# Small softmax operations of a second expert folded and given to GpSimd, its pairs written in another order

## The chip, the cores and the metric

The kernel runs on one core of a Trainium2 chip. A core has a matrix engine (TensorE, PE in the profile), a vector engine (VectorE, DVE), a scalar engine (ScalarE, ACT), a general engine (GpSimd, POOL) and an engine that here only starts DMAs (SyncE, SP). Each works through its own list of instructions in the order in which they were written, and waits for the others by semaphores. PE accumulates in PSUM, eight banks of 512 fp32 columns for 128 partitions. The metric is the device time of one execution in microseconds, lower is better.

## The reference

Three stages follow one another: linear attention, a first expert `h * cos(h)`, and the second expert that the change touches:

```python
def _moe2_ref(x, w_in, w_out, g_ln):          # x: 4608 x 512
    h = x @ w_in                              # 512 x 1024
    e = np.exp(h - np.max(h, axis=-1, keepdims=True))
    sm = e / (np.sum(e, axis=-1, keepdims=True) + 1e-09)
    solu = h * sm
    mu = np.mean(solu, axis=-1, keepdims=True)
    var = np.mean((solu - mu) ** 2, axis=-1, keepdims=True)
    ln = (solu - mu) / np.sqrt(var + 1e-06) * g_ln
    return (ln @ w_out).astype(np.float32)    # 1024 x 512
```

All is fp32, for 4608 tokens. The softmax's division by z, the sum of the exponentials, is never carried out: h times e is normalised as it stands, and the small constants are scaled by the square of z.

## The kernel before

Matrix products in fp32 precision are made from split numbers: each operand is a high part (rounded, ACT's cast at L479) and a low part (what is left, POOL's or DVE's subtraction at L480), and `mm3` (L204 to L206) adds three matmuls. Products of two by two blocks use seven block products instead of eight, with sums of blocks as operands.

The second expert works on 18 pairs of 128-token tiles, u = 0 to 17. For a pair:
- `prep_second` loads x (L1188), makes block sums on POOL (L779) and splits them (L479 on ACT, L480 on POOL).
- `second` (S below) makes h by seven products of six matmuls of 512 columns. `H_SEED[u]` chooses one of three ways to combine the products: by DVE sums (L1231), by DVE operations that add and take the row maximum at once (L1236), and by ACT copies (L1241, L1281, L1288).
- `soft` runs once for each of the two tiles, n = 0 and 1 ("rows"): the negated maximum `nmx` (L1309, DVE), Exp with its sum z (L1314, ACT), h times e with its sum (L1317, DVE), the negated mean `nmp` (L1320, DVE), the square of z (L1324, ACT), the squared deviations with their sum (L1326, ACT), the variance (L1328, DVE), its power -1/2 (L1331, POOL), a product (L1345, POOL) and the normalisation (L1347, ACT).
- `permute` writes the result through DMAs (L1365, SP), `turned` transposes it and splits it (L1392, L1403, L1415, L1416), all on engines beside PE; pairs 0 and 17 have PE transposes.
- `second_out` (O below) makes the output by seven products. Where `O_WIDE[u]` is set and u is under 16, a product is four pairs of matmuls of 512 and 256 columns (L1466, L1468); else it is twelve matmuls of 256 (L204 to L206). ACT copies (L1483, L1500), DVE sums (L1476, L1490, L1496) and POOL sums (L1492) combine them, and DMAs write them out (L1583).

So that PE always has work, the products of S for one pair stand between products of O for a pair two places earlier. In a flow of such pairs an output product's accumulation bank is copied by ACT (`ps<-ps` copies at L1483 and L1500) before PE opens the third output product in the bank that the copy frees or fills.

The order of every engine is not written by hand. Each `add` in the functions notes an operation with its engine, a planned duration, what it reads and writes, and a priority `at`. `Flow.run` then plans them all: it takes the operation that could start first, among those the one of lowest `at`, and calls its function, which issues the instruction. DVE and POOL operations that are not marked `ps` never overlap in that plan. The tables at the head of the file (leads and lags in us, `H_SEED`, `O_WIDE`, `O_SEED`) set the priorities and the forms:

```python
            t = min((t for t in q if start(t) <= s), key=lambda t: (t.at, t.seq))
            q.remove(t)
            ...
            t.fn()
```

The functions are stored as lambdas and run here, after all the `add` calls of all pairs have been made.

Of the kernel before, what the change touches and what calls it, by code (L numbers as in the profile page):

```python
# [53 lines left out]
E2_LEAD, SOFT_AT, SOFT_D, Q_OFF, CP_D = -33.18, -44.29, -15.08, -0.17, 6.96  # L54
# [5 lines left out]
S_A1, S_AL, S_DL, E2_AT, S_BL, ITEM_L, ACC_AT = -19.57, 38.93, 58.24, 168.95, 35.39, 38.61, -6.64  # L60
# [6 lines left out]
PREP_LO, P1_SEED, CHAIN_POOL, H_SEED, O_SEED = (1, 1, 1, 1), (1, 1, 1, 1, 0, 0, 1, 0, 0, 1, 0, 1, 0, 0, 1), (0,), (2, 2, 0, 0, 0, 2, 0, 0, 2, 0, 0, 0, 0, 0, 0, 0, 0, 0), (2, 0, 1, 0, 1, 1, 2, 1, 1, 0, 0, 1, 0, 0, 0, 0, 2, 1)  # L67
STRASSEN = (0, 0, 0, 0, 1, 0, 1, 1, 0, 1, 1, 0, 1, 1, 1)
O_WIDE, MM_W = (0, 0, 1, 0, 0, 1, 1, 1, 1, 0, 1, 1, 0, 1, 0, 0, 0, 1), 0.342
# [123 lines left out]
def tile_kernel(ctx, tc, qkv, tail, g2, w1, w2, gl, out):  # L193
# [1106 lines left out]
    def soft(u, n, at):  # L1300
# [4 lines left out]
        def sm(name):  # L1305
            return buf[name, n]

        if n or H_SEED[u] != 1:
            add("DVE", 0.15, lambda: DVE.tensor_scalar(out=sm("nmx"), in0=sm("mb"), scalar1=-1.0, scalar2=None,  # L1309
                                                       op0=ALU.mult), r=[("mb", n)], w=[("nmx", n)], at=at, ps=True)  # L1310
        else:
            add("DVE", 1.19, lambda: DVE.tensor_reduce(out=sm("nmx"), in_=buf[hk], axis=AX.X, op=ALU.max, negate=True),
                r=[*halves], w=[("nmx", n)], at=at, ps=True)
# [3 lines left out]
        add("DVE", 1.3, lambda: DVE.scalar_tensor_tensor(out=buf[hk], in0=buf[hk], scalar=1.0, in1=buf[ek],  # L1317
                                                          op0=ALU.mult, op1=ALU.mult, accum_out=sm("sp")),
            r=[*halves, ek], w=[hk, ("sp", n)], at=at)
        add("DVE", 0.15, lambda: DVE.tensor_scalar(out=sm("nmp"), in0=sm("sp"), scalar1=-1.0 / FP, scalar2=None,  # L1320
                                                  op0=ALU.mult), r=[("sp", n)], w=[("nmp", n)], at=at, ps=True)


        add("ACT", 0.27, lambda: ACT.activation(out=sm("zz"), in_=sm("z"), func=AF.Square, scale=1e-3,  # L1324
                                               bias=buf["halfpi"][:, 1:2]), r=[("z", n), "tiny"], w=[("zz", n)], at=at)
        add("ACT", 1.24, lambda: ACT.activation(out=buf["junk"], in_=buf[hk], func=AF.Square, bias=sm("nmp")[:, 0:1],  # L1326
                                                accum_out=sm("v")), r=[hk, ("nmp", n)], w=[("v", n), "junk"], at=at)
        add("DVE", 0.16, lambda: DVE.scalar_tensor_tensor(out=sm("v"), in0=sm("v"), scalar=1.0 / FP, in1=sm("zz"),  # L1328
                                                         op0=ALU.mult, op1=ALU.add),
            r=[("v", n), ("zz", n)], w=[("v", n)], at=at)  # L1330
# [12 lines left out]

        if n in NORM_ACT:
            add("POOL", 0.2, lambda: POOL.tensor_tensor(out=sm("nmp"), in0=sm("nmp"), in1=sm("ry"), op=ALU.mult),  # L1345
                r=[("ry", n)], w=[("nmp", n)], at=at, ps=True)
            add("ACT", 1.13, lambda: ACT.activation(out=normed(), in_=plain(), func=AF.Identity, scale=sm("ry")[:, 0:1],  # L1347
                                                   bias=sm("nmp")[:, 0:1]),
                r=[hk, ("nmp", n), ("ry", n)], w=[("nx", n)], at=at)
            return  # L1350
# [587 lines left out]
```

## Time and profile before

| what | value |
|---|---|
| time, median of 3 runs (lowest to highest) | 1195.18 us (1194.14 to 1196.62) |
| the profiled execution, and its span | 1195.32 us, 1193.4 us |
| PE, DVE, ACT, POOL busy, share of the span | 99%, 79%, 72%, 62% |
| granted TensorE clock, mean | 0.998 of full speed |

The second expert's pairs fill about the last 350 us. A busy share is an average over three stages, and the end of a matmul in the profile is modelled, so pauses of PE are read below from the starts of successive matmuls. In the timeline a row has the start, the duration, the engine, the line, the operation and its tiles, and in brackets the idle time before it with the operation that ended it; two rows of equal kind are joined, with x2.

### The profile page before, as it was taken

What the parts mean: (1) busy time and instruction counts of PE and PEld (TensorE: products, weight loads), DVE (VectorE), ACT (ScalarE), POOL (GpSimd) and SP (SyncE); (2) the same over time, 40 slices, a digit from 0 to 9 for tenths busy, and PEclk for the clock granted to TensorE, in tenths of its full rate; (3) what the DMA queues carried; (4) which work ended last, traced back from release to release, by engine and by line L of the source; (5) the groups of instructions that cost most, each with busy time, mean ns of one, the idle gap of its engine ahead of it and who ended that gap; (6) DMA issues with size and microseconds to landing.
All of it is one profiled execution on the core that took longest, in us unless ns stands there. A gap on an engine that the chain in (4) does not pass through costs nothing.

```text
span 1193.4 us, 20361 instructions
## 1 busy us (share of the span) xinstructions
PE 1177.4 (99%) x6678; PEld 1023.4 (86%) x6678; DVE 945.2 (79%) x1631; ACT 861.8 (72%) x1602; POOL 740.8 (62%) x737
## 2 busy tenths in 40 slices
PE   7999999999999999999999999999999999999998
PEld 6788888888999999888888878888898988888898
DVE  6877666666657769789989888887789888989895
ACT  6787777777655746767577758664879878787874
POOL 3377675667534345778477646877567675776732
PEclk9999999999999999999999999999999999999999
DMA  9899999988967987986598569879834342433331
GB/s 321 287 364 330 332 319 326 327 271 302 306 200 215 316 275 228 354 302 219 179 353 313 202 206 336 283 247 333 275 108 117 92 134 79 131 100 100 102 94 54
DMA packets 244394, 281.35 MB, mean 236 GB/s; under 512 B 17984, under 2 KB 169536, under 8 KB 244288
## 3 DMA queue, kind: packets, MB, share of 16 engines
q1 hardware_dynamic: 244288, 280.04, 72.2%
q8 instruction: 53, 0.87, 0.3%
q14 instruction: 53, 0.43, 0.1%
HBM read 184.03 MB, written 79.17 MB: 221 GB/s over the span
## 4 chain that ended last, share of the span: by engine, by line
PE 90%; DVE 5%; SPq 2%; ACT 1%; DMA 1%; issue 1%; POOL 0%; DVEq 0%; ACTq 0%
PE ps L204 26%; PE ps L206 26%; PE ps L205 26%; PE ps L1466 4%; PE ps L709 3%; PE ps L1468 2%; PE ps L591 2%; SPq L1365 1%; PE ps L741 1%; DMA att<-qkv 1%; DMA xf<-px 1%; DVE mid L1084 0%; DVE rxa L480 0%; DVE ps L1392 0%; DVE fconv L1403 0%
## 5 line engine op out<-in xcount | busy, mean ns | idle before, releaser
L204 PE MATMUL ps<-rg,rwo 128*128 128x512 f32 (+2 forms) x752 | 269.6, 359 | 2.0 <-DVE fh L1084 1.1
L206 PE MATMUL ps<-rg,rwo 128*128 128x512 f32 (+2 forms) x752 | 265.7, 353 | 0.0
L205 PE MATMUL ps<-rg,rwo 128*128 128x512 f32 (+2 forms) x752 | 265.5, 353 | 0.0
L204 PEld LDWEIGHTS ps<-rg,rwo 128*128 128x128 f32 x752 | 141.7, 188 | 20.7 <-DVE mid L1084 2.7
L206 PEld LDWEIGHTS ps<-rg,rwo 128*128 128x128 f32 x752 | 141.7, 188 | 16.3
L480 POOL TENSOR_TENSOR rg<-rawp,rg 128x512 fp32r<-128x512 f32 (+1 forms) x84 | 116.8, 1402 | 62.0 <-ACT rg L479 58.4
L205 PEld LDWEIGHTS ps<-rg,rwo 128*128 128x128 f32 x752 | 141.9, 189 | 15.0
L204 PE MATMUL ps<-rxa,rwi 128*128 128x512 f32 (+1 forms) x384 | 144.8, 377 | 0.0
L206 PE MATMUL ps<-rxa,rwi 128*128 128x512 f32 (+1 forms) x384 | 144.3, 376 | 0.0
L205 PE MATMUL ps<-rxa,rwi 128*128 128x512 f32 (+1 forms) x384 | 144.3, 376 | 0.0
L840 DVE SCALAR_TENSOR_TENSOR fh<-ps,fh 128x512 f32<-128x512 f32 (+1 forms) x126 | 81.0, 648 | 45.7 <-ACT fh L838 44.0
L843 ACT ACTIVATE fh<-fh,const 128x512 f32<-128x512 f32 (+1 forms) x156 | 105.1, 689 | 16.7 <-DVE fh L840 15.6
L204 PE MATMUL ps<-rxb,rwi 128*128 128x512 f32 (+1 forms) x288 | 109.4, 380 | 1.9 <-DVE fh L948 0.9
L205 PE MATMUL ps<-rxb,rwi 128*128 128x512 f32 (+1 forms) x288 | 108.4, 376 | 0.0
L206 PE MATMUL ps<-rxb,rwi 128*128 128x512 f32 (+1 forms) x288 | 108.3, 376 | 0.0
L480 POOL TENSOR_TENSOR ws<-fconv,ws 128x512 fp32r<-128x512 f32 x68 | 83.3, 1228 | 38.6 <-ACT ws L479 32.7
L479 ACT CAST rg<-rawp 128x512 fp32r<-128x512 f32 (+1 forms) x144 | 83.3, 597 | 27.3 <-PE ps L206 18.9
L838 ACT ACTIVATE fh<-ps 128x512 int32<-128x512 f32 (+1 forms) x126 | 70.6, 566 | 44.1 <-PE ps L206 41.8
L779 POOL TENSOR_TENSOR sf<-xf 128x256 f32<-128x256 f32 x72 | 65.5, 909 | 30.5 <-DMA xf<-xd 22.8
L204 PEld LDWEIGHTS ps<-rxa,rwi 128*128 128x128 f32 x384 | 72.1, 188 | 12.1 <-ACT ps L963 0.4
L206 PEld LDWEIGHTS ps<-rxa,rwi 128*128 128x128 f32 x384 | 72.1, 188 | 11.7
L205 PEld LDWEIGHTS ps<-rxa,rwi 128*128 128x128 f32 x384 | 72.1, 188 | 10.8
(197 smaller groups left out, 3122.1 us busy)
## 6 DMA issues: line engine op xcount, KB each, us to landing
rwi<-wid SPq DMA_DIRECT2D x66, 512.0 KB, 6.0
rwo<-wod SPq DMA_DIRECT2D x104, 256.0 KB, 4.4
att<-qkv SPq DMA_DIRECT2D x32, 512.0 KB, 6.2
rwo<-wsd SPq DMA_DIRECT2D x32, 512.0 KB, 5.3
fh<-e2n SPq DMA_DIRECT2D x256, 64.0 KB, 2.1
fconv<-w SPq DMA_DIRECT2D x28, 512.0 KB, 5.4
px<-fh SPq DMA_DIRECT2D x42, 256.0 KB, 5.3
xd<-xf SPq DMA_DIRECT2D x18, 512.0 KB, 5.3
```

Of the source, the lines that this page charges most:

```text
L204: PE.matmul(ps, lhsT=lh, rhs=rh, start=start, stop=False, skip_group_check=more)
L205: PE.matmul(ps, lhsT=lh, rhs=rl, start=False, stop=False, skip_group_check=more)
L206: PE.matmul(ps, lhsT=ll, rhs=rh, start=False, stop=stop, skip_group_check=more)
L479: add("ACT", 0.62 if n == 512 else 0.405, lambda: ACT.copy(out=hi(), in_=src()), r=keys, w=hk, at=at)
L480: either(on_dve, n, lambda eng: eng.tensor_tensor(out=lo(), in0=src(), in1=f(hi()), op=ALU.subtract), [*keys, *hk], lk, at)
L591: PE.matmul(buf[bk][e * D:(e + 1) * D, p % 2 * D:(p % 2 + 1) * D], lhsT=k_[:, at_:at_ + D], rhs=k_[:, v_ + at_:v_ + at_ + D], start=(c == ...
L709: PE.matmul(buf[bk][row:row + n, c], lhsT=buf[qs[p]][:, a:a + n], rhs=buf[kvf][:, c], start=True, stop=True)
L779: add("POOL", 0.74, lambda: POOL.tensor_tensor(out=out_(), in0=in0(), in1=in1(), op=fn), r=[*keys, *r], w=w, at=at)
L838: add("ACT", e_(0.6, 0.385, n), lambda: ACT.activation(out=tt().bitcast(I32), in_=h(), func=AF.Copy, scale=INV_2PI, bias=0.25), r=r, w=[tk ...
L840: add("DVE", e_(0.69, 0.418, n), lambda: DVE.scalar_tensor_tensor(out=tt(), in0=h(), scalar=INV_2PI, in1=tt().bitcast(I32), op0=ALU.mult, ...
L843: add("ACT", e_(0.725, 0.509, n), lambda: ACT.activation(out=tt(), in_=tt(), func=AF.Sin, bias=buf["halfpi"][:, 0:1], scale=TWO_PI), r=[tk ...
L1466: PE.matmul(buf[bk], lhsT=hi, rhs=lw_room(b, c // 2)[:, c % 2, :], start=first, stop=False, skip_group_check=True)
```

## The change

Four things are edited in the second expert.
- The mean is no operation of its own any more: the product h times e carries the factor 1/1024, so that its sum is the mean; the squared deviations take it as bias with scale -1024, and POOL's product makes the negated, scaled mean from it.
- The square of z goes from one ACT operation to two on POOL, the variance from DVE to POOL. `SMALL_POOL` holds a flag each for nmx, the square of z and the variance: (0, 1, 1).
- `H_SEED` sets the form with ACT copies alone (1) for pairs 7 and 8, where the first row's nmx is a reduction over 1024 columns on DVE, and form 2 for pairs 0, 1 and 14 (before: 0, 1, 5 and 8). `O_WIDE` chooses pairs 2, 3, 5, 7, 10, 11, 12, 14 (before: 2, 5, 6, 7, 8, 10, 11, 13).
- Leads and lags of the pairs have other values. Two places declare a change of owner of the normalised rows' buffers (pairs 1 and 17).

PE issues 6185 matmuls in both programs; DVE 1597 and now 1476 instructions, ACT 1532 and 1507, POOL 742 and 884, SP 1078 and 1078.

```diff
-E2_LEAD, SOFT_AT, SOFT_D, Q_OFF, CP_D = -33.18, -44.29, -15.08, -0.17, 6.96
+E2_LEAD, SOFT_AT, SOFT_D, Q_OFF, CP_D = -28.65, -4.13, -11.15, -0.17, 6.96
...
-PREP_LO, P1_SEED, CHAIN_POOL, H_SEED, O_SEED = (1, 1, 1, 1), (1, 1, 1, 1, 0, 0, 1, 0, 0, 1, 0, 1, 0, 0, 1), (0,), (2, 2, 0, 0, 0, 2, 0, 0, 2, 0, 0, 0, 0, 0, 0, 0, 0, 0), (2, 0, 1, 0, 1, 1, 2, 1, 1, 0, 0, 1, 0, 0, 0, 0, 2, 1)
+PREP_LO, P1_SEED, CHAIN_POOL, H_SEED, O_SEED = (1, 1, 1, 1), (1, 1, 1, 1, 0, 0, 1, 0, 0, 1, 0, 1, 0, 0, 1), (0,), (2, 2, 0, 0, 0, 0, 0, 1, 1, 0, 0, 0, 0, 0, 2, 0, 0, 0), (2, 0, 1, 1, 1, 1, 1, 1, 1, 0, 1, 1, 1, 2, 2, 0, 1, 0)
-O_WIDE, MM_W = (0, 0, 1, 0, 0, 1, 1, 1, 1, 0, 1, 1, 0, 1, 0, 0, 0, 1), 0.342
+O_WIDE, MM_W = (0, 0, 1, 1, 0, 1, 0, 1, 0, 0, 1, 1, 1, 0, 1, 0, 0, 0), 0.342
...
-PAIR_C, DMA_LAG, TURN_LAG, OUT_LAG = 58.48, 33.18, 71.85, 121.5
-NORM_ACT = (0, 1)
+PAIR_C, DMA_LAG, TURN_LAG, OUT_LAG = 45.03, 67.83, 45.54, 113.17
 PERM_T = 0.45
-S4_POOL, TAIL, TAIL_LAG = 0, 2, -3.08
-H_EV, XT_LAG, O_EV, LAST_DVE, LAST_TR, FIRST_TR = 136.78, 35.72, 165.16, 18, -65.4, 45.07
+SMALL_POOL = (0, 1, 1)
+S4_POOL, TAIL, TAIL_LAG = 0, 2, -113.56
+H_EV, XT_LAG, O_EV, LAST_DVE, LAST_TR, FIRST_TR = 147.46, 51.63, 195.18, 18, 5.8, 8.07
...
         if n or H_SEED[u] != 1:
-            add("DVE", 0.15, lambda: DVE.tensor_scalar(out=sm("nmx"), in0=sm("mb"), scalar1=-1.0, scalar2=None,
-                                                       op0=ALU.mult), r=[("mb", n)], w=[("nmx", n)], at=at, ps=True)
+            eng, dur = ("POOL", 0.2) if SMALL_POOL[0] else ("DVE", 0.15)
+            add(eng, dur, lambda: (POOL if eng == "POOL" else DVE).tensor_scalar(
+                out=sm("nmx"), in0=sm("mb"), scalar1=-1.0, scalar2=None, op0=ALU.mult),
+                r=[("mb", n)], w=[("nmx", n)], at=at, ps=True)
...
-        add("DVE", 1.3, lambda: DVE.scalar_tensor_tensor(out=buf[hk], in0=buf[hk], scalar=1.0, in1=buf[ek],
+        add("DVE", 1.3, lambda: DVE.scalar_tensor_tensor(out=buf[hk], in0=buf[hk], scalar=1.0 / FP, in1=buf[ek],
                                                           op0=ALU.mult, op1=ALU.mult, accum_out=sm("sp")),
             r=[*halves, ek], w=[hk, ("sp", n)], at=at)
-        add("DVE", 0.15, lambda: DVE.tensor_scalar(out=sm("nmp"), in0=sm("sp"), scalar1=-1.0 / FP, scalar2=None,
-                                                  op0=ALU.mult), r=[("sp", n)], w=[("nmp", n)], at=at, ps=True)
-
-
-        add("ACT", 0.27, lambda: ACT.activation(out=sm("zz"), in_=sm("z"), func=AF.Square, scale=1e-3,
-                                               bias=buf["halfpi"][:, 1:2]), r=[("z", n), "tiny"], w=[("zz", n)], at=at)
-        add("ACT", 1.24, lambda: ACT.activation(out=buf["junk"], in_=buf[hk], func=AF.Square, bias=sm("nmp")[:, 0:1],
-                                                accum_out=sm("v")), r=[hk, ("nmp", n)], w=[("v", n), "junk"], at=at)
-        add("DVE", 0.16, lambda: DVE.scalar_tensor_tensor(out=sm("v"), in0=sm("v"), scalar=1.0 / FP, in1=sm("zz"),
-                                                         op0=ALU.mult, op1=ALU.add),
-            r=[("v", n), ("zz", n)], w=[("v", n)], at=at)
+        if SMALL_POOL[1]:
+            def eps():
+                POOL.tensor_scalar(out=sm("zz"), in0=sm("z"), scalar1=1e-3 / FP, scalar2=1e-12 / FP, op0=ALU.mult, op1=ALU.add)
+                POOL.tensor_tensor(out=sm("zz"), in0=sm("zz"), in1=sm("zz"), op=ALU.mult)
+
+            add("POOL", 0.4, eps, r=[("z", n)], w=[("zz", n)], at=at, ps=True)
+        else:
+            add("ACT", 0.27, lambda: ACT.activation(out=sm("zz"), in_=sm("z"), func=AF.Square, scale=1e-3 / FP,
+                                                   bias=buf["halfpi"][:, 1:2]), r=[("z", n), "tiny"], w=[("zz", n)], at=at)
+        add("ACT", 1.24, lambda: ACT.activation(out=buf["junk"], in_=buf[hk], func=AF.Square, scale=-float(FP),
+                                                bias=sm("sp")[:, 0:1], accum_out=sm("v")),
+            r=[hk, ("sp", n)], w=[("v", n), "junk"], at=at)
+
+        def var(eng):
+            return lambda: eng.tensor_scalar(out=sm("v"), in0=sm("v"), scalar1=1.0 / FP ** 3, scalar2=sm("zz")[:, 0:1],
+                                             op0=ALU.mult, op1=ALU.add)
+
+        eng, dur = ("POOL", 0.2) if SMALL_POOL[2] else ("DVE", 0.16)
+        add(eng, dur, var(POOL if SMALL_POOL[2] else DVE), r=[("v", n), ("zz", n)], w=[("v", n)], at=at, ps=True)
         add("POOL", 0.56, lambda: POOL.tensor_tensor(out=sm("ry"), in0=sm("v"), in1=buf["mhalf"][:, 0:1], op=ALU.pow),
             r=[("v", n), "mhalf"], w=[("ry", n)], at=at)
+
+        if n == 0 and u in (1, NU - 1):
+            nx = [("nx", i) for i in range(2)]
+            flow.change(lambda: None, nx, nx)
 
         def normed():
             if u in (0, NU - 1):
@@ -1341,15 +1355,11 @@
                 return buf[hk]
             return buf[hk].rearrange("p (k c i) -> p k c i", c=4, i=32)
 
-        if n in NORM_ACT:
-            add("POOL", 0.2, lambda: POOL.tensor_tensor(out=sm("nmp"), in0=sm("nmp"), in1=sm("ry"), op=ALU.mult),
-                r=[("ry", n)], w=[("nmp", n)], at=at, ps=True)
-            add("ACT", 1.13, lambda: ACT.activation(out=normed(), in_=plain(), func=AF.Identity, scale=sm("ry")[:, 0:1],
-                                                   bias=sm("nmp")[:, 0:1]),
-                r=[hk, ("nmp", n), ("ry", n)], w=[("nx", n)], at=at)
-            return
-        add("DVE", 0.83, lambda: DVE.tensor_scalar(out=normed(), in0=buf[hk], scalar1=sm("nmp")[:, 0:1],
-                                                   scalar2=sm("ry")[:, 0:1], op0=ALU.add, op1=ALU.mult),
+        add("POOL", 0.2, lambda: POOL.tensor_scalar(out=sm("nmp"), in0=sm("sp"), scalar1=sm("ry")[:, 0:1], scalar2=-1.0 / FP,
+                                                    op0=ALU.mult, op1=ALU.mult),
+            r=[("ry", n), ("sp", n)], w=[("nmp", n)], at=at, ps=True)
+        add("ACT", 1.13, lambda: ACT.activation(out=normed(), in_=plain(), func=AF.Identity, scale=sm("ry")[:, 0:1],
+                                               bias=sm("nmp")[:, 0:1]),
             r=[hk, ("nmp", n), ("ry", n)], w=[("nx", n)], at=at)
```

The places in the built programs on which the rest of the text rests follow. First POOL around the softmax of pair 12: `rwi` are the split operands of the next products, `sf` the block sums, `xf` the loaded x, `const` the one-column numbers, `edge` the row maxima. Before:

```order
L480 TENSOR_TENSOR rwi_0_731<-sf_108,rwi_0_731 128x512
L480 TENSOR_TENSOR rwi_0_731<-xf_113,rwi_0_731 128x512
L779 TENSOR_TENSOR sf_107<-xf_112 128x256
L480 TENSOR_TENSOR rwi_0_731<-sf_108,rwi_0_731 128x512
L779 TENSOR_TENSOR sf_107<-sf_107,xf_112 128x256
L779 TENSOR_TENSOR sf_107<-xf_112 128x256
L779 TENSOR_TENSOR sf_107<-xf_112,sf_107 128x256
L480 TENSOR_TENSOR rwi_0_731<-xf_113,rwi_0_731 128x256
L1331 TENSOR_TENSOR const_73<-const_73,const_70 128x1
```

and now:

```order
L480 TENSOR_TENSOR rwi_0_731<-sf_108,rwi_0_731 128x512
L480 TENSOR_TENSOR rwi_0_731<-xf_113,rwi_0_731 128x512
L1310 TENSOR_SCALAR const_73<-edge_133 128x1
L480 TENSOR_TENSOR rwi_0_731<-sf_108,rwi_0_731 128x512
L1310 TENSOR_SCALAR const_73<-edge_133 128x1
L1324 TENSOR_SCALAR const_73<-const_73 128x1
L1325 TENSOR_TENSOR const_73<-const_73 128x1
L480 TENSOR_TENSOR rwi_0_731<-xf_113,rwi_0_731 128x256
L1324 TENSOR_SCALAR const_73<-const_73 128x1
L1325 TENSOR_TENSOR const_73<-const_73 128x1
```

The rows at L1310 are nmx of the two rows: `eng`, which the lambda at L1311 reads when the plan runs, has been set again in the same call of `soft`, from "DVE" by the first flag to "POOL" by the third. L1324 and L1325 are the square of z. In all of POOL's list L1310 stands 34 times, 32 of them right behind an operation over the full width (24 an L480 of 512 columns, the others an L779 or L1426); DVE's list has none.

Second, ACT at the same place: `fconv` are the rows of h and their Exps, `ps_0_169` a PSUM bank. Before:

```order
L479 CAST rwi_0_731<-xf_113 128x512
L1415 CAST e2r_7847<-ps_0_189 128x512
L479 CAST rwi_0_731<-sf_108 128x512
L1314 ACTIVATE fconv_103,const_73<-fconv_103,const_73 128x1024
L1324 ACTIVATE const_73<-const_73,const_69 128x1
L1314 ACTIVATE fconv_103,const_73<-fconv_103,const_73 128x1024
L1500 COPY ps_0_169<-ps_0_173 128x512
L1324 ACTIVATE const_73<-const_73,const_69 128x1
L1326 ACTIVATE fconv_103,const_73<-fconv_103,const_73 128x1024
```

and now, where Exp has the line 1316 and the copy 1510:

```order
L479 CAST rwi_0_731<-xf_113 128x512
L479 CAST rwi_0_731<-sf_108 128x512
L1316 ACTIVATE fconv_103,const_73<-fconv_103,const_73 128x1024
L479 CAST rwi_0_731<-xf_113 128x256
L1316 ACTIVATE fconv_103,const_73<-fconv_103,const_73 128x1024
L1510 COPY ps_0_169<-ps_0_173 128x512
L1331 ACTIVATE fconv_103,const_73<-fconv_103,const_73 128x1024 x2
```

The square of z is gone from between the Exps, a cast of 256 columns stands there instead, and the bank's copy is behind both Exps as it was. Of the new order's other pairs, 10 has the same form with a copy of 256 columns (L1493), 4, 5, 9, 14 and 16 have Exp, cast, copy, Exp, and 13 has Exp, copy, Exp. One of these, ACT in pair 9, before:

```order
L1288 COPY fconv_103<-ps_0_173 128x512
L479 CAST rwi_0_731<-xf_112 128x512
L479 CAST rwi_0_731<-sf_107 128x512
L1415 CAST e2r_7847<-ps_0_189 128x512
L1314 ACTIVATE fconv_103,const_73<-fconv_103,const_73 128x1024
L1500 COPY ps_0_169<-ps_0_197 128x512
L1314 ACTIVATE fconv_103,const_73<-fconv_103,const_73 128x1024
L1324 ACTIVATE const_73<-const_73,const_69 128x1 x2
L1326 ACTIVATE fconv_103,const_73<-fconv_103,const_73 128x1024
L1500 COPY e2n_7451<-ps_0_169 128x512
```

and now:

```order
L1288 COPY fconv_103<-ps_0_173 128x512
L479 CAST rwi_0_731<-xf_112 128x512
L1425 CAST e2r_7844<-ps_0_189 128x512
L479 CAST rwi_0_731<-sf_107 128x512
L1316 ACTIVATE fconv_103,const_73<-fconv_103,const_73 128x1024
L479 CAST rwi_0_731<-xf_112 128x256
L1510 COPY ps_0_169<-ps_0_197 128x512
L1316 ACTIVATE fconv_103,const_73<-fconv_103,const_73 128x1024
L1331 ACTIVATE fconv_103,const_73<-fconv_103,const_73 128x1024
L1510 COPY e2n_7451<-ps_0_169 128x512
```

The copy of the bank has a cast of 256 columns ahead of it, which the list of before has at another place, and the cast of the block sums (`sf`) now stands right in front of the first Exp.

## Rows read from the trace of the kernel before

**Rows 1.** The page's head and its first part: busy time, share, instructions.

```profile
span 1193.4 us, 20361 instructions
...
PE 1177.4 (99%) x6678; PEld 1023.4 (86%) x6678; DVE 945.2 (79%) x1631; ACT 861.8 (72%) x1602; POOL 740.8 (62%) x737
```

**Rows 2.** Timeline of PE at 860 us: start, duration, operation [idle, releaser].

```profile
860.23 0.39 PE L205 MATMUL ps<-rxa,rwi 128*128 128x512 f32 x1
860.46 0.39 PE L206 MATMUL ps<-rxa,rwi 128*128 128x512 f32 x1
861.51 0.50 PE L204 MATMUL ps<-rxb,rwi 128*128 128x512 f32 x1 [0.67 <-DVE edge L1236]
861.85 0.39 PE L205 MATMUL ps<-rxb,rwi 128*128 128x512 f32 x1
```

**Rows 3.** Timeline of PE at 1117 us.

```profile
1116.98 0.28 PE L1468 MATMUL ps<-rg,rwo 128*128 128x256 f32 x1
1117.40 0.50 PE L204 MATMUL ps<-rxb,rwi 128*128 128x512 f32 x1
1117.74 0.40 PE L205 MATMUL ps<-rxb,rwi 128*128 128x512 f32 x1
```

**Rows 4.** Lines by form, 811 to 1194 us: operation xcount, busy us, mean ns, idle.

```profile
L1328 DVE SCALAR_TENSOR_TENSOR const<-const 128x1 f32<-128x1 f32 x36 | 7.0, 202 | 4.1 <-ACT fconv L1326 3.9
...
L479 ACT CAST rwi<-xf 128x256 fp32r<-128x256 f32 x17 | 6.8, 403 | 0.7 <-PE ps L205 0.7
L1345 POOL TENSOR_TENSOR const<-const 128x1 f32<-128x1 f32 x36 | 6.8, 190 | 2.8
...
L1309 DVE TENSOR_SCALAR const<-edge 128x1 f32<-128x1 f32 x36 | 5.4, 153 | 1.2
...
L1320 DVE TENSOR_SCALAR const<-const 128x1 f32<-128x1 f32 x36 | 5.2, 151 | 2.6
```

**Rows 5.** Timeline of pair 12's softmax, 1057.6 to 1063.4 us.

```profile
1057.96 0.39 PE L206 MATMUL ps<-rxa,rwi 128*128 128x512 f32 x1
...
1058.86 1.30 POOL L480 TENSOR_TENSOR rwi<-sf,rwi 128x512 fp32r<-128x512 f32 x1
...
1059.18 0.15 DVE L1309 TENSOR_SCALAR const<-edge 128x1 f32<-128x1 f32 x1
...
1059.45 1.16 ACT L1314 ACTIVATE fconv<-fconv,const 128x1024 f32<-128x1024 f32 x1 [0.67 <-DVE const L1309]
...
1060.93 1.14 ACT L1314 ACTIVATE fconv<-fconv,const 128x1024 f32<-128x1024 f32 x1
...
1062.07 0.58 ACT L1500 COPY ps<-ps 128x512 f32<-128x512 f32 x1
...
1063.07 0.40 PE L1466 MATMUL ps<-rg,rwo 128*128 128x512 f32 x1
```

**Rows 6.** Timelines of POOL and L1309 at pairs 4, 10 and 16.

```profile
903.66 2.56 POOL L480 TENSOR_TENSOR rwi<-sf,rwi 128x512 fp32r<-128x512 f32 x2
904.38 0.22 DVE L1309 TENSOR_SCALAR const<-edge 128x1 f32<-128x1 f32 x2
...
1019.87 2.54 POOL L480 TENSOR_TENSOR rwi<-sf,rwi 128x512 fp32r<-128x512 f32 x2
1020.09 0.15 DVE L1309 TENSOR_SCALAR const<-edge 128x1 f32<-128x1 f32 x1
...
1137.32 1.31 POOL L480 TENSOR_TENSOR rwi<-sf,rwi 128x512 fp32r<-128x512 f32 x1 [0.66 <-ACT rwi L479]
1138.00 0.15 DVE L1309 TENSOR_SCALAR const<-edge 128x1 f32<-128x1 f32 x1
```

**Rows 7.** Timeline of POOL and DVE in pair 12, at its first L1317.

```profile
1060.11 0.74 POOL L779 TENSOR_TENSOR sf<-sf,xf 128x256 f32<-128x256 f32 x1
...
1060.73 1.23 DVE L1317 SCALAR_TENSOR_TENSOR fconv<-fconv 128x1024 f32<-128x1024 f32 x1
1060.80 1.75 POOL L779 TENSOR_TENSOR sf<-xf 128x256 f32<-128x256 f32 x1
```

More of the change, by code (lines that the diff above doesn't have):

```diff
@@ L59 @@
 S_A, S_B, S_D = 39.3, 27.7, 11.68
-S_A1, S_AL, S_DL, E2_AT, S_BL, ITEM_L, ACC_AT = -19.57, 38.93, 58.24, 168.95, 35.39, 38.61, -6.64
+S_A1, S_AL, S_DL, E2_AT, S_BL, ITEM_L, ACC_AT = -19.57, 32.84, 112.35, 198.17, 54.28, 38.61, -6.64
 PREP_LEAD, PREP_D, H_LATE, H_EARLY, JOB_AT = 8.61, 11.37, -85.04, -0.19, 8.82
@@ L1603, in tile_kernel @@
                                            stop=True), r=["ident"], w=[BANKS[0]], at=-50)
-    add("DVE", 0.1, lambda: DVE.memset(buf["halfpi"][:, 1:2], 1e-12), w=["tiny"], at=300)
+    add("DVE", 0.1, lambda: DVE.memset(buf["halfpi"][:, 1:2], 1e-12 / FP), w=["tiny"], at=300)
     add("DVE", 0.1, lambda: DVE.memset(buf["halfpi"][:, 2:3], 0.0), w=["zero"], at=301)
```

## The prediction

> **What bounds the kernel now.** I read the page first: TensorE (PE) is busy 99% of a span of 1193.4 us, GpSimd (POOL) 62% [rows 1]. Time can thus leave only through pauses of PE, for the built program issues the same 6185 matmuls over the same columns, and the same ones up to 818.5 us of the trace of before and again from 1154 us to the end. So I read the PE timeline of the stretch between, matmul start by matmul start. Its pitch is 0.23 us for 512 columns (860.23 to 860.46 [rows 2]), 0.12 for 256, and 0.35 for an output product's 512+256 pair (1057.96 to 1063.07 holds ten of 512 and eight pairs, (5.11 - 10 x 0.23) / 8 [rows 5]). Three pauses exceed 0.3 us. At 860.46 the next matmul starts 1.05 us later and the one after it 0.34 later, 0.82 + 0.11 = 0.93 us lost, put down to VectorE's (DVE's) combining operation L1236, which had not emptied the accumulation bank [rows 2]. At 1116.98 the next start is 0.42 us away where 0.12 is due, and again 0.11 is lost on the second matmul: 0.41 [rows 3]. The one between, at 901 us, gives 0.46 by the same reading. Together 1.80 us. That is about the most that a new order of this stretch can win; two smaller pauses of 0.2 us each are left out.
>
> Then I read a softmax. The lines view prices its small operations: DVE's negated maximum (nmx, L1309) 153 ns, mean L1320 151, variance L1328 202, POOL's one-column product L1345 190 [rows 4]. The timeline of pair 12 shows the chain [rows 5]: the last matmul of the sixth product starts at 1057.96 (call this t0), nmx at 1059.18, the Exp at 1059.45 = t0 + 1.49, the second Exp at 1060.93, the copy of the output product's bank L1500 at 1062.07 for 0.58, and PE opens the third output product, which needs that bank, at 1063.07. The copy ends at 1062.65: 0.42 us to spare. ScalarE (ACT) idled 0.67 us for L1309 before that first Exp, so this chain has no slack between t0 and the Exp.
>
> **The change part by part.** *DVE loses work.* 36 L1320 (5.2 us), 36 L1328 (7.0 us) and 34 of the 36 L1309 (5.4 x 34/36 = 5.1 us) go: 17.3 us of DVE [rows 4]. None was on PE's path except through L1236's lateness, so I count their worth inside the pauses above. *ACT loses* the square of z; ACT lies beside PE: nothing by itself. *POOL gains* 34 nmx, 72 operations for z's square, 36 for the variance, and its 36 products stay in another form: 142 more at about 0.19 us [rows 4] is 27 us on an engine with 38% of the span idle [rows 1]. Behind the Square of pair u the results are needed only by output products that stand two pairs of PE work later, which the pitch makes 42 x 0.23 + 28 x 0.35 = 19.5 us each; a row's extra 3 x 0.19 = 0.6 us is hidden there, and would cost that much a row if it were not. *SP's DMAs and the two extra changes of buffer owner* move inside the same cover: nothing. *The tail's PE order* is unchanged: nothing.
>
> *The wait that is new.* nmx is planned on DVE for 0.15 us, but its operation is made when the plan runs, after `eng` has been set again, and the order shows it issued on POOL. There it stands behind whatever POOL was given just before: 32 of 34 stand right behind a full-width operation, 24 of them a 128x512 low split (L480). How late is it? In before I take the moment of each first-row L1309 and ask how much of POOL's running operation is left. Pair 12: L480 from 1058.86 to 1060.16, L1309 at 1059.18: 0.98 us left [rows 5]. Of the thirteen pairs 4 to 16 the first gives 903.66 + 1.30 - 904.38 = 0.58, the last 1137.32 + 1.31 - 1138.00 = 0.63, the largest, pair 10 with two operations in its row, 1019.87 + 1.27 - 1020.09 = 1.05 [rows 6]; the mean by this reading is 0.76. So the wait r lies between 0 (POOL idle, or its operations earlier) and 1.05, and I take 0.76, because the new order puts the same kind of operation at the same place.
>
> What queues behind a late Exp on ACT: in eight pairs the new order has the copy of the output bank behind one or two Exps, and PE's third output product waits for it. With Exp 1.15 (1062.07 - 1060.93 is 1.14 [rows 5]), a cast of 256 columns 0.40, the copy of 512 columns 0.58 (one of 256 taken as the cast, 0.40) [rows 4, 5] and 0.05 for the hop: pairs 4, 5, 9, 14 (Exp, cast, copy): t0 + 1.49 + 1.15 + 0.40 + 0.58 + 0.05 = t0 + 3.67. PE gets there after 7 matmuls and 8 pairs, 1.61 + 2.80 = 4.41: 0.74 to spare. Pair 16 has one pair fewer in between: 0.39. Pair 10 (Exp, cast, Exp, 0.40 copy) t0 + 4.64 against 10 matmuls of 512 and 24 of 256, 5.18: 0.54. Pair 12 (Exp, cast, Exp, 0.58 copy) t0 + 4.82 against the 5.11 of before, whose PE order here is the same: 0.29. Pair 13 (Exp, copy) t0 + 3.27 against 13 matmuls and 4 pairs, 4.39: 1.12. With r = 0.76: 4 x 0.02 + 0.37 + 0.22 + 0.47 + 0 = 1.14 us, and each of the seven pauses brings the 0.11 us on its second matmul that rows 2 show: 0.77. In all 1.9 us. With r = 0 nothing; with r = 1.05 it is 4 x 0.31 + 0.66 + 0.51 + 0.76 = 3.17, + 0.77 = 3.9 us.
>
> *The reordered steps.* The three old pauses sit at places that no longer exist in this form (-1.80). Others of their kind can arise: between 0 and again 1.80. I take the smallest of the three, 0.41, as DVE is lighter.
>
> *Sum:* profiled execution 1195.32 (span 1193.4 and 1.9 around it) - 1.80 + 0.41 + 1.9 = 1195.8. The median of the runs is 0.14 lower than the profiled one: **1195.7 us**.
>
> *A rule that speaks against the change.* In pair 12 POOL's L779 takes 0.74 us at 1060.11 and 1.75 at 1060.80, while DVE's L1317, with two inputs in SBUF, runs from 1060.73 [rows 7]. The Trainium skill, "GPSIMD Engine Reference", § 8 Key points, says that GpSimd shares its SBUF interfaces with VectorE and contends with DVE instructions that have two SBUF inputs. The trace agrees; by this rule POOL's small operations, the second row's nmx among them, can be held beside L1317, which the fourth rival prices from the rows.
>
> **The rivals.**
> 1. *The lateness is absorbed*: POOL, though it has more to do, is ahead of its plan when nmx comes, r near 0.1 (ACT's 0.67 us of waiting before the Exp stays as it is). For it: POOL idles a third of the span. Against it: POOL was running a full operation at all thirteen places read. 1195.32 - 1.80 + 0.41 - 0.14 = 1193.8; with no pause at all 1193.4, and with the two small ones gone too 1193.0.
> 2. *nmx waits a full operation* (the slower side): r is 1.05 or more at every pair, because the L480 in front starts only when ACT's cast, itself just before the Exp, has ended; four pairs, 9, 11, 13 and 16, have that cast right in front of the Exp. It decides from r above 0.74, where the four pairs with equal margin join in earnest. 1195.32 - 1.80 + 0.41 + 3.9 - 0.14 = 1197.7; with the old pauses back in full 1199.1.
> 3. *The rebuilt order has worse pauses of the old kind*: three or four more L1236-like waits of 0.93 beyond those removed, 1195.32 + 4 x 0.93 - 0.14 = 1198.9. Against it: DVE is 17 us lighter.
> 4. *Contention on top*: each second-row nmx that falls beside L1317 is late by the 1.0 us that L779 lost; it matters where the copy is behind the second Exp, pairs 10 and 12: 1195.7 + 2 x 1.0 = 1197.7.
>
> **How the numbers follow.** The forecast, 1194.8 to 1197.2, has 0.46; rival 1 has 0.24, rival 2 0.15, rival 3 0.05, rival 4 0.10. That one wide measurement separates from no change is taken as 0.2%, 2.4 us: faster means under 1192.8, slower over 1197.6. Faster holds only the edge of rival 1 and what the smaller pauses and unread stretches could add: 0.08. Slower holds most of rivals 2 to 4, 0.24, and 0.06 of the forecast's upper side: 0.30. The rest, 0.62, is the same within 0.2%. The range runs from 1193.1 (rival 1 with nearly every pause gone) to 1198.9 (rivals 2 and 4 with room for an old pause or two).
>
> **What would show it.** Right: nmx on POOL in the lines view, 34 times, and ACT's wait before the Exp put down to POOL and longer than the 0.67 us of [rows 5]; Exp at about t0 + 2.2; PE pauses of 0.1 to 0.6 us at the third output product of pairs 10, 12 and 16, with an ACT copy of a bank as the releaser; none at 860 and 1117 us behind L1236; the last matmul about 0.7 us later. Wrong: PE pauses at other places or behind DVE, or none at all; Exp at t0 + 1.5 as before; a gain beyond 2.4 us would mean pauses in stretches I took as full.

## The result and the profile after

The changed kernel takes 1201.26 us in the median of six runs (1199.88 to 1203.54) against 1195.31 for the kernel before on the same chip: a ratio of 1.0056, 95% interval 1.0045 to 1.0068. Run again later on another chip it came to 1.0067 (1.0054 to 1.0080). The ratios here and below are those on record; they can differ a little from the quotient of two medians, which is 1.0050 for the first. It is slower by some 6 us, above the predicted range.

The page's head and first part, to be read beside [rows 1]:

```profile
span 1200.1 us, 20360 instructions
...
PE 1181.2 (98%) x6678; PEld 1023.5 (85%) x6678; DVE 921.8 (77%) x1510; ACT 858.8 (72%) x1577; POOL 792.8 (66%) x879
```

DVE is 23 us lighter, POOL 52 us heavier, and the span 6.7 us longer. I add up PE's pauses as in the prediction: from the starts of successive matmuls behind 815 us, what exceeds the pitch by over 0.05 us. Before it is 2.9 us, now 9.9, 7.0 more: the whole loss is pauses of PE in the second expert. The view of waits of PE from 811 us to the end names what ended them (waited for: us in total, times, longest):

```profile
PE ps L204 <- ACT e2n L1493: 1.5, 2, 1.0
PE ps L1476 <- ACT ps L1510: 0.8, 2, 0.5
PE ps L204 <- DVE edge L1236: 0.6, 2, 0.4
PE ps L1390 <- ACT e2n L1361: 0.5, 1, 0.5
PE ps L204 <- ACT ps L1241: 0.4, 1, 0.4
PE ps L1476 <- ACT e2n L1510: 0.3, 1, 0.3
```

Before, this view had one line:

```profile
PE ps L204 <- DVE edge L1236: 0.9, 2, 0.7
```

Now five of six releasers are on ACT: copies of banks, and a normalisation (L1361). (The view counts idle time from the modelled end of the matmul before, so it names 4.1 of the 9.9 us.) So the next view is ACT's own waits, after:

```profile
ACT fconv L1316 <- POOL const L1310: 15.5, 16, 1.8
...
ACT e2n L1361 <- POOL const L1358: 11.3, 19, 1.1
```

and before:

```profile
ACT fconv L1314 <- DVE const L1309: 12.4, 16, 2.7
...
ACT e2n L1347 <- POOL const L1345: 0.5, 2, 0.3
```

The wait for nmx before Exp grew by 3 us, that of the normalisation for its last small operation on POOL (L1358) from 0.5 to 11.3 us. Against the kernel before the second is the larger change; against the same order with nothing on POOL (7.0 and 2.9 us, in the table below) the two grew alike, to 15.9 and 12.9. The lines view by form, from 811 us, answers to [rows 4]:

```profile
L1361 ACT ACTIVATE e2n<-fconv,const 128x1024 f32<-128x1024 f32 x36 | 44.8, 1244 | 12.9 <-POOL const L1358 11.3 <-DMA xf<-px 1.4
...
L1316 ACT ACTIVATE fconv<-fconv,const 128x1024 f32<-128x1024 f32 x36 | 41.4, 1151 | 15.9 <-POOL const L1310 15.5 <-POOL rwo L1426 0.3
...
L1324 POOL TENSOR_SCALAR const<-const 128x1 f32<-128x1 f32 x36 | 28.1, 781 | 5.7 <-ACT fconv L1316 3.1
...
L1325 POOL TENSOR_TENSOR const<-const 128x1 f32<-128x1 f32 x36 | 13.2, 366 | 3.0
...
L1336 POOL TENSOR_SCALAR const<-const 128x1 f32<-128x1 f32 x36 | 10.8, 300 | 5.1 <-ACT fconv L1331 1.7
...
L1310 POOL TENSOR_SCALAR const<-edge 128x1 f32<-128x1 f32 x34 | 9.6, 283 | 11.4 <-DVE edge L1236 5.7 <-DVE edge L1257 5.4
```

L1310 is nmx, 34 times on POOL as the order said. The square of z (L1324, L1325) takes 1.15 us a row (0.781 + 0.366) where the plan gave 0.4. The timeline of pair 12 answers to [rows 5]:

```profile
1063.22 0.24 POOL L1310 TENSOR_SCALAR const<-edge 128x1 f32<-128x1 f32 x1 [1.13 <-DVE edge L1236]
...
1063.49 1.16 ACT L1316 ACTIVATE fconv<-fconv,const 128x1024 f32<-128x1024 f32 x1 [0.77 <-POOL const L1310]
...
1064.77 1.23 DVE L1319 SCALAR_TENSOR_TENSOR fconv<-fconv 128x1024 f32<-128x1024 f32 x1
1064.85 1.21 POOL L1310 TENSOR_SCALAR const<-edge 128x1 f32<-128x1 f32 x1
...
1066.09 1.15 ACT L1316 ACTIVATE fconv<-fconv,const 128x1024 f32<-128x1024 f32 x1 [1.06 <-POOL const L1310]
...
1067.24 0.58 ACT L1510 COPY ps<-ps 128x512 f32<-128x512 f32 x1
...
1067.87 0.50 PE L1476 MATMUL ps<-rg,rwo 128*128 128x512 f32 x1 [0.47 <-ACT ps L1510]
```

The second row's nmx begins just after DVE's two-input L1319 and lasts as long as that, 1.21 us; Exp, the bank's copy and the third output product follow late. In pair 4 the second row's nmx is held in the same way, and a copy and an output product follow late there too (0.54 us):

```profile
906.12 2.09 DVE L1319 SCALAR_TENSOR_TENSOR fconv<-fconv 128x1024 f32<-128x1024 f32 x1
...
907.08 1.20 POOL L1310 TENSOR_SCALAR const<-edge 128x1 f32<-128x1 f32 x1
...
908.31 1.16 ACT L1316 ACTIVATE fconv<-fconv,const 128x1024 f32<-128x1024 f32 x1 [1.45 <-POOL const L1310]
...
911.21 0.50 PE L1476 MATMUL ps<-rg,rwo 128*128 128x512 f32 x1 [0.25 <-ACT e2n L1510]
```

The other kind is seen in pair 15:

```profile
1128.77 1.15 ACT L1331 ACTIVATE fconv<-fconv,const 128x1024 bf16<-128x1024 f32 x1
...
1132.29 0.74 POOL L779 TENSOR_TENSOR sf<-xf 128x256 f32<-128x256 f32 x1
...
1133.14 0.27 POOL L1336 TENSOR_SCALAR const<-const 128x1 f32<-128x1 f32 x1
...
1133.49 0.55 POOL L1341 TENSOR_TENSOR const<-const,const 128x1 f32<-128x1 f32 x1
...
1134.14 0.26 POOL L1358 TENSOR_SCALAR const<-const 128x1 f32<-128x1 f32 x1
...
1134.44 1.24 ACT L1361 ACTIVATE e2n<-fconv,const 128x1024 f32<-128x1024 f32 x1 [1.06 <-POOL const L1358]
...
1135.59 0.35 ACT L1493 COPY e2n<-ps 128x256 f32<-128x256 f32 x1
...
1135.99 0.50 PE L204 MATMUL ps<-rxb,rwi 128*128 128x512 f32 x1 [1.00 <-ACT e2n L1493]
```

The second row's Square ends at 1129.92, its variance begins on POOL 3.2 us later, behind splits, a sum and the first row's own small operations, which POOL was given first. ACT stands 1.06 us before the normalisation, and the copy of an output bank, which has nothing to do with it, is next in ACT's list. PE loses 1.27 us.

Every pause over 0.2 us can be followed back in the timeline in this way, from releaser to releaser. Seven, at 848, 882, 914, 958, 1075, 1113 and 1136 us, lead to a normalisation that waited for L1358, some through further operations on ACT and DVE: 3.9 us. Four, of pairs 4, 9, 12 and 16, lead to an Exp that waited for nmx: 2.1 us.

### The profile page after: what moved, and what is told of

The parts are those of the page before. It is cut to its first block, busy times and chain, and to the rows that moved or that the text cites. A ratio compares the mean times of both kernels' runs of the same rounds, so it can differ in the third digit from the quotient of the medians.

```text
span 1200.1 us, 20360 instructions
## 1 busy us (share of the span) xinstructions
PE 1181.2 (98%) x6678; PEld 1023.5 (85%) x6678; DVE 921.8 (77%) x1510; ACT 858.8 (72%) x1577; POOL 792.8 (66%) x879
## 4 chain that ended last, share of the span: by engine, by line
PE 81%; POOL 7%; DVE 4%; ACT 4%; issue 3%; SPq 1%; DMA 1%; POOLq 0%; DVEq 0%; ACTq 0%
PE ps L204 24%; PE ps L205 23%; PE ps L206 23%; PE ps L1476 3%; PE ps L709 3%; POOL rwi L480 2%; PE ps L591 2%; PE ps L1478 2%; PE ps L741 1%; ACT e2n L1361 1%; SPq L1375 1%; POOL sf L779 1%; POOL const L1341 1%; POOL const L1324 1%; DMA att<-qkv 1%
## 5 line engine op out<-in xcount | busy, mean ns | idle before, releaser
L480 POOL TENSOR_TENSOR rg<-rawp,rg 128x512 fp32r<-128x512 f32 (+1 forms) x84 | 115.9, 1392 | 63.0 <-ACT rg L479 61.3
L480 POOL TENSOR_TENSOR ws<-fconv,ws 128x512 fp32r<-128x512 f32 x68 | 83.9, 1238 | 38.7 <-ACT ws L479 32.3
L204 PEld LDWEIGHTS ps<-rxa,rwi 128*128 128x128 f32 x384 | 72.1, 188 | 13.1 <-ACT ps L1241 0.9
L462 POOL TENSOR_TENSOR fconv<-fconv 128x512 int32<-128x512 int32 x40 | 54.1, 1352 | 43.3 <-DVE fconv L455 37.0
L206 PEld LDWEIGHTS ps<-rxa,rwi 128*128 128x128 f32 x384 | 72.1, 188 | 11.6
L1084 DVE TENSOR_TENSOR mid<-ps,mid 128x512 f32<-128x512 f32 (+1 forms) x104 | 67.5, 658 | 18.1 <-PE ps L206 17.2
```

What stands on the lines that cost most here:

```text
L204: PE.matmul(ps, lhsT=lh, rhs=rh, start=start, stop=False, skip_group_check=more)
L206: PE.matmul(ps, lhsT=ll, rhs=rh, start=False, stop=stop, skip_group_check=more)
L462: add("POOL", 1.3, lambda: POOL.tensor_tensor(out=buf[wk].bitcast(I32), in0=buf[yk].bitcast(I32), in1=buf[wk].bitcast(I32), op=ALU.add), r ...
L480: either(on_dve, n, lambda eng: eng.tensor_tensor(out=lo(), in0=src(), in1=f(hi()), op=ALU.subtract), [*keys, *hk], lk, at)
L1084: add("DVE", e_(0.69, 0.418, n), lambda ak=ak, bk=bk: DVE.tensor_tensor(out=buf[ak][:, 0:n], in0=buf[bk][:, 0:n], in1=buf[ak][:, 0:n], op= ...
```

## Experiments

Most edits here leave the plan alone and change only the engine that an operation is issued to, so that every other engine's order stays as it was. The table holds all that kept the changed kernel's plan: the ratio to the kernel before on the same chip, PE's pauses reckoned as above, and ACT's idle time before the Exps and before the normalisations (lines view).

| what differs from the changed kernel | ratio (95% interval) | PE pauses | before Exp | before norm. |
|---|---|---|---|---|
| (the kernel before) | 1 | 2.9 | 12.7 | 0.9 |
| nothing | 1.0067 (1.0054 to 1.0080) | 9.6 | 15.9 | 12.6 |
| nmx on DVE | 1.0008 (0.9999 to 1.0017) | 4.3 | 7.4 | 7.7 |
| variance on DVE | 1.0013 (1.0005 to 1.0022) | 4.5 | 13.5 | 4.8 |
| square of z on ACT | 1.0017 (1.0008 to 1.0026) | 5.1 | 13.9 | 2.9 |
| all three off POOL | 0.9999 (0.9990 to 1.0008) | 2.7 | 7.0 | 2.9 |
| only nmx on POOL | 1.0016 (1.0007 to 1.0025) | 5.3 | 13.7 | 3.5 |
| square of z later on POOL | 1.0079 (1.0064 to 1.0093) | 11.2 | 16.0 | 15.4 |
| normalisation later on ACT | 1.0035 (1.0023 to 1.0048) | 7.9 | 14.3 | 2.5 |
| all off POOL, norm. delayed | 1.0363 (1.0347 to 1.0380) | 46.6 | 8.2 | 50.9 |

**The three operations, one by one.** nmx back on DVE, which is one word:

```diff
-            add(eng, dur, lambda: (POOL if eng == "POOL" else DVE).tensor_scalar(
+            add(eng, dur, lambda eng=eng: (POOL if eng == "POOL" else DVE).tensor_scalar(
```

> The changed kernel with one word more: nmx keeps the engine that its plan gave it (DVE); every engine's order is otherwise the same. Changed kernel: 1201.3 us, 9.9 us of PE pauses behind 815 us. Theory A (the late nmx is the root; the Exp waits 15.5 us in all for it, and the normalisation is late because the Exp was): the wait goes, PE pauses fall by 4 to 5 us, 1196 to 1197. Theory B (two roots: nmx, and the chain square of z, variance, power, product on POOL, for which ACT's normalisation waits 11.3 us): only the pauses at the third output products of pairs 4, 9, 12 and 16 go, 0.54 + 0.21 + 0.75 + 0.62 = 2.1 us, 1199; ACT's wait for L1358 stays near 11 us. Theory C (the new order itself): under 1 us.

Measured 1.0008. The variance on DVE:

```diff
-        add(eng, dur, var(POOL if SMALL_POOL[2] else DVE), r=[("v", n), ("zz", n)], ...
+        add(eng, dur, var(DVE), r=[("v", n), ("zz", n)], ...
```

> The changed kernel with the variance issued on DVE where the plan has it on POOL; nmx and the square of z stay on POOL. Theory B: ACT's wait for L1358 falls well under 11.3 us and with it the pauses behind a late normalisation (847, 914, 1075, 1113 and 1135 us, 0.73 + 0.33 + 0.27 + 0.22 + 1.27 = 2.8 us): 1198.5. Theory A: nothing, 1201, since the variance is late only as the Exp is. Theory C: nothing.

Measured 1.0013. Theory A foresaw the first and is refuted by the second; theory B's sum of two parts falls too, since each edit alone gave back over 5 of the 7 us. All three off POOL (both edits, and the square of z as in the third below):

> The changed kernel with all three small operations issued off POOL (nmx and variance on DVE, square of z as one ACT operation), the plan and all orders otherwise those of the change. Theories A and B: both groups of pauses go, 4.9 us, 1196.3. Theory C (the new tables are the cause): still 1200 or more. What is left over 1195.3 is the part of the new order: by the trace of the changed kernel pauses of 1.7 us behind L1236 and about 1.5 us at pairs 2, 3 and 7, where the old order had 1.8 us in all.

Measured 0.9999, pauses 2.7 us: the new order is as good as the old one, and theory C is out for this plan. The changed kernel again, then the square of z alone:

> The changed kernel once more, beside the next three on one chip, since each single undoing gave back most of the 6 us. If the loss belongs to the kernel: a ratio near 1.0056 and 9 to 10 us of PE pauses behind 815 us. If the first chip or its moment made part of it: 1.002 to 1.004, and pauses of 5 to 7 us.

Measured 1.0067: it is the kernel's, with nearly the same pauses at the same places.

```diff
-                POOL.tensor_scalar(out=sm("zz"), in0=sm("z"), scalar1=1e-3 / FP, scalar2=1e-12 / FP, ...
-                POOL.tensor_tensor(out=sm("zz"), in0=sm("zz"), in1=sm("zz"), op=ALU.mult)
+                ACT.activation(out=sm("zz"), in_=sm("z"), func=AF.Square, scale=1e-3 / FP, bias=buf["halfpi"][:, 1:2])
```

> The changed kernel with only the square of z issued on ACT, as one operation, instead of two on POOL; nmx and variance stay on POOL. In the changed kernel 23 of the 36 first operations of that square took about 1.05 us instead of 0.19, all begun while DVE's two-input product L1319 ran. Theory D (a POOL operation that begins beside L1319 is held until it ends, and POOL's queue behind it is late): the holds go, POOL is 40 us less busy, PE pauses fall from 9.9 to about 5, ratio 1.001 to 1.002. Theory A (nmx behind a full operation is the root): the Exp waits as before (15 us), pauses 8 or more, ratio 1.004 or more.

Measured 1.0017, with the Exp waiting as long as ever (13.9 us): again most of the loss gone. That agreed with theory D, so I took the hold away and left the work on POOL, by issuing the two operations in front of the variance:

```diff
+            def run():
+                eps()
+                eng.tensor_scalar(out=sm("v"), in0=sm("v"), scalar1=1.0 / FP ** 3, scalar2=sm("zz")[:, 0:1], ...
```

> The changed kernel with the square of z issued on POOL as before, two operations, but right in front of the variance instead of right behind the Exp: POOL has the same operations and the same plan, only these two stand later in its list. Theory D (the loss needs the hold beside L1319): held operations fall from 34 to under 10, PE pauses from 9.6 us to 5 to 6, ratio 1.001 to 1.003. Theory E (the loss is POOL's added number of operations, whatever they stand beside): holds may fall but the pauses stay at 8 or more, ratio 1.005 or more, as the chain to the normalisation is longer by 2 x 0.19 us.

Measured 1.0079. Operations of one column over 0.7 us fell from 34 to 18, as wanted, and the time rose. Theory D is refuted; it had not fitted the variance's run either, which has 33 held operations left and lost 5 us of its pauses. Theory E, the count of operations, foresaw this run but not the three before it, where taking off a quarter of the 142 operations (or half, the square of z) gave back two thirds of the loss or more. The table has a better reading: the wait before the normalisation grew to 15.4 us, as the chain from Square to it is longer by the two operations.

**Exp or normalisation.** Only nmx on POOL, the rest off it:

> The orders of the change with only nmx issued on POOL (variance on DVE, square of z on ACT). ACT's idle time before Exp should be about 14 us, before the normalisation about 3. Theory F (PE pauses follow the sum of ACT's waits before Exp, Square and normalisation in the new order: 12.9 us gave 2.7 us of pauses, 20.2 gave 4.3, 32.6 gave 9.9): about 18 us of waits, 4 to 5 us of pauses, ratio 1.001 to 1.002. Theory A (nmx makes most of the loss): 8 us or more, ratio 1.004 or more.

Measured 1.0016 with 5.3 us of pauses, 2.6 more than with nothing on POOL: theory A is out, theory F came near. The lines view of this run:

```profile
L1360 ACT ACTIVATE e2n<-fconv,const 128x1024 f32<-128x1024 f32 x36 | 44.5, 1241 | 3.5 <-POOL const L1357 3.3
...
L1316 ACT ACTIVATE fconv<-fconv,const 128x1024 f32<-128x1024 f32 x36 | 41.3, 1148 | 13.7 <-POOL const L1310 13.5 <-POOL rwo L1425 0.2
```

The opposite, Exp on time and the normalisation late, by six idle operations that multiply by 1:

```diff
+            for _ in range(6):
+                POOL.tensor_scalar(out=sm("ry"), in0=sm("ry"), scalar1=1.0, scalar2=1.0, op0=ALU.mult, op1=ALU.mult)
             POOL.tensor_scalar(out=sm("nmp"), in0=sm("sp"), scalar1=sm("ry")[:, 0:1], scalar2=-1.0 / FP, ...
```

> All small operations off POOL as in the run with 2.7 us of pauses, but six idle operations of one column put on POOL between the power and the last product of each row, some 1.2 to 1.6 us: the normalisation alone is late, Exp is not. Theory F: ACT waits 15 us or more for the normalisation, about 25 in all, pauses 5 to 6 us, ratio 1.002 to 1.003. Theory G (it needs both the late Exp and the late normalisation): pauses under 4 us, ratio up to 1.001.

```profile
L1364 ACT ACTIVATE e2n<-fconv,const 128x1024 f32<-128x1024 f32 x36 | 44.8, 1243 | 50.9 <-POOL const L1360 50.9
...
L1316 ACT ACTIVATE fconv<-fconv,const 128x1024 f32<-128x1024 f32 x36 | 41.3, 1148 | 8.2 <-DVE const L1310 8.0
```

Measured 1.0363. I was wrong in size by far: 48 us more of waiting before the normalisation brought 44 us more of PE pauses, nearly one for one. Theory G is refuted: the late normalisation alone is enough. (The six operations also keep POOL busy for 42 us, and POOL idled 50 us for the variance, so some of its other work may be late as well. Followed back as above, pauses of 33.7 of the 46.6 us lead to a normalisation that waited for POOL.) Last, the waiting kept and the work behind it let past:

```diff
-            t.fn()
+            if getattr(t, "late", False):       # the normalisation: hold it back by one ACT instruction
+                ...
```

> The changed kernel with 30 of the 36 normalisations issued one place later on ACT, so that the next copy or cast goes ahead of the one that waits for POOL; everything on POOL stays. Theory F' (what hurts is the work queued behind the waiting normalisation on ACT): pauses fall from 9.6 us to 5 to 7, ratio 1.002 to 1.004. If the normalisation's lateness hurts through what reads it, or POOL's own queue is the cause: 9 us or more, ratio 1.006 or more.

Measured 1.0035, half the loss back (1.0067 to 1.0035), pauses 7.9 us, above the 5 to 7 expected. What ACT then runs before the normalisation partly waits itself: the pauses that lead back to a waiting normalisation fell from 3.3 us to 1.3, the others grew from 6.3 to 6.7. This is only partial support.

**The old order and new plans.** nmx on POOL in the kernel before, then the square of z:

```diff
-            add("DVE", 0.15, lambda: DVE.tensor_scalar(out=sm("nmx"), in0=sm("mb"), ...
+            add("DVE", 0.15, lambda: POOL.tensor_scalar(out=sm("nmx"), in0=sm("mb"), ...
```

> The kernel before with nmx issued on POOL where the plan has it on DVE, nothing else. By the prediction's step on nmx: margins of the bank copies 0.39 to 0.9 us against 0.76 of wait give 1.9 us plus 0.11 for each of some seven pauses: 1197.9. Theory A (nmx alone makes most of the 6 us): 1199 to 1201. Theory C: no more than 1196.

```diff
-        add("ACT", 0.27, lambda: ACT.activation(out=sm("zz"), in_=sm("z"), func=AF.Square, scale=1e-3, ...
+        add("ACT", 0.27, eps, r=[("z", n), "tiny"], w=[("zz", n)], at=at)      # eps: the two operations on POOL
```

> The kernel before with only the square of z issued on POOL, as two operations at its old place behind the Exp, plan unchanged. Theory D: 20 or more operations held beside L1317; POOL's list is about 1 us late a row, the low splits and the normalisation with it: ratio 1.0015 to 1.004. Theory C or E: 72 x 0.19 us more on POOL, hidden: ratio 1.000 to 1.001, with few long operations.

Measured 1.0011 (1.0001 to 1.0020) and 0.9996 (0.9987 to 1.0005). In the first, Exp waits 19.7 us instead of 12.7, the normalisation 1.0, and pauses come to 4.5 us: about half of what I expected of nmx in the old order. The second has 20 held operations and loses nothing: a second refutation of theory D. Four kernels were planned anew:

```diff
-SMALL_POOL = (0, 1, 1)
+SMALL_POOL = (1, 1, 1)
```

> SMALL_POOL = (1, 1, 1): nmx is now also planned on POOL, where the changed kernel issued it, so that the planner orders the other work round it. Theory A: the wait of ACT for nmx falls and with it the pauses behind it; ratio 1.001 to 1.003. Theory D: the plan knows nothing of the hold beside L1319, so the square of z is held as before; ratio 1.003 or more, and no fewer operations of over 0.7 us.

> The new softmax (nmx, variance, square of z on POOL as the change issues them) under the tables of the kernel before: forms, leads and lags as they were. Theory C (new tables): about as before, ratio 1.000 to 1.001. Theories A and D: the small operations on POOL cost here too, 3 to 6 us, ratio 1.0025 to 1.005.

> SMALL_POOL = (0, 0, 0) in the changed kernel: nmx and variance planned and issued on DVE, the square of z on ACT, and all orders planned anew from the new tables. The fold of the mean stays. If POOL's small operations make the whole loss: ratio 0.999 to 1.001. If the new tables cost by themselves: 1.002 or more.

> The same, SMALL_POOL = (0, 0, 0), under the tables of the kernel before: the fold of the mean alone, 36 operations of 0.15 us less on DVE. If DVE's lateness behind L1236 is what pauses PE in the kernel before, 0.5 to 1.5 us go, ratio 0.9985 to 0.9995; if the new order that the plan finds has its own pauses, 1.000 to 1.003.

Measured 1.0093, 1.0128, 1.0042 and 1.0036, with pauses of 12.8, 17.4, 8.6 and 6.0 us. The last two have nothing more on POOL than the kernel before and still lose 4 to 5 us: a plan made anew by tables that do not belong to it moves the time by as much as the change did, so these four do not price the operations.

**A version under both.** The fold of the mean alone, by leaving its DVE operation out of the issued order of the kernel before:

```diff
-        add("DVE", 0.15, lambda: DVE.tensor_scalar(out=sm("nmp"), in0=sm("sp"), scalar1=-1.0 / FP, ...
+        add("DVE", 0.15, lambda: None, r=[("sp", n)], w=[("nmp", n)], at=at, ps=True)
```

> The kernel before with the mean's operation on DVE left out of the issued order and folded into scales as the change does, plan and tables unchanged. Pauses 2.9 us before; DVE is 5.4 us lighter, so those behind L1236 (1.8 us) may shrink: 2 to 2.9 us, ratio 0.999 to 1.000 under every theory; the version most likely to be under both kernels.

Measured 0.9986 (0.9978 to 0.9995), 1193.61 against 1195.00 us. Its waits of PE from 818 us:

```profile
PE ps L204 <- DVE edge L1236: 0.6, 1, 0.6
```

Pauses 2.1 us. Of the three old ones behind L1236 that at 860 us stays (0.87), those at 901 and 1117 us are gone.

## Why the prediction was wrong

- **The step that failed** is "POOL gains": "Behind the Square of pair u the results are needed only by output products that stand two pairs of PE work later", "hidden there". The data are needed that late, but ACT waits for them at once: the normalisation stands in ACT's list a few instructions behind the Square, and bank copies stand behind it. I asked who reads the result and not what is queued behind the instruction that waits. The step was priced at nothing; on top of nmx, which has 2.6 us of pauses alone, the variance and the square of z bring 4.3 (9.6 - 5.3), without nmx 1.6 (4.3 - 2.7). The 142 more operations themselves took 61.7 us (9.6 + 28.1 + 13.2 + 10.8), not 27. That late normalisations pause PE is shown, by the run that delays them and by the pauses that lead back to them: 3.9 us in the changed kernel, 1.8 with nmx on DVE, 0.5 with the square of z on ACT, 0.2 with nmx alone on POOL, none over 0.2 us with the variance on DVE. That the three parts do not add (any one taken off gives back 4.5 to 5.3 us) fits one chain in which only what exceeds its slack is paid, and this is argued, not shown.
- **nmx** was right in part, and its sum came out near by luck. The pauses behind late Exps were those of pairs 4, 9, 12 and 16, 0.54 + 0.21 + 0.75 + 0.62 = 2.1 us against 1.9 for all pairs; pairs 10, 5 and 14 had none. Pairs 9 and 16 (0.83 us) have the cause that I had priced, a first row's nmx behind a full-width operation; pairs 4 and 12 (1.29 us) have my fourth rival's, the second row's nmx held beside L1319. The wait was over-sized: the first Exps (11 pairs from 4 to 16) began 1.78 us on average behind the modelled end of the sixth product, and 1.29 with nmx on DVE, so 0.49 later where I took 0.76.
- **The reordered steps** were put at -1.80 + 0.41. With nothing on POOL the new order has 2.7 us of pauses against 2.9: two of 0.72 and 0.75 us at 869 and 902 us, the first behind a copy on ACT, the second behind L1236, stand where I had counted one of 0.41. The gain was 0.2, not 1.4.
- **DVE's relief** shows no gain in the changed kernel: pauses behind L1236 there (at 882, 904, 1042 and 1062 us) come to 1.7 us, that at 882 by way of a late normalisation, against 1.8 before. No run undoes the fold in the new order; in the old one the fold's 5.2 us [rows 4] bought 0.8 us of pauses.
- **The rivals.** The second had the right side, but for Exp alone; its long wait came in the four pairs that it named, 9, 11, 13 and 16 (first Exp 0.6 to 1.1 us later than with nmx on DVE), not in all. The fourth came true twice, in pairs 4 and 12. No rival was about the normalisation, so the range missed the time by 2.4 us.
- **Signs.** nmx on POOL 34 times and PE's pauses at 860 and 1117 us gone were right, as were pauses at pairs 12 and 16; pair 10 had none, and pair 12's first Exp stood at t0 + 1.6, not 2.2; "the last matmul about 0.7 us later" was ten times too small.

## What to carry to other kernels

When an operation moves to an engine with a long list, price the instruction that waits for it by everything queued behind that instruction on its own engine, not by when its result is read. Change the issuing engine and the plan in separate runs: a plan made anew can move the time by more than the edit. A function that is stored and run later reads its variables then; look at which engine the built program has.

## What the runs showed of the hardware

Of 214 one-column operations of POOL in this stage of the changed kernel 34 took over 0.7 us, most about 1.05 to 1.2 instead of 0.19 to 0.27, and all 34 began while DVE's two-input L1319 ran; in the kernel before none of 72 did, and none began there. The Trainium skill, "GPSIMD Engine Reference", § 8 Key points, names such contention for DVE instructions with two SBUF inputs, and the trace agrees. What I had not expected is how little it can cost: 20 such long operations in the old order, 19 of them begun beside L1317, left the time where it was. In the changed kernel the two that were an nmx are followed by 1.29 us of pauses; what the other 32 cost there no run isolates. The hold goes both ways: of the 36 L1319 the 11 that took over 1.3 us, up to 2.09 where 1.23 is usual, all began while POOL ran an operation of 256 or 512 columns, and so did all 16 such L1317 in the kernel before.
